# Another order of the action list in a one-core RetNet attention and GELU MLP kernel

## The chip, the core and the metric

The kernel runs on one core of a Trainium2 chip. The metric is the device time of one execution in microseconds (us). The profiler records one execution: every instruction of the engines PE (TensorE matmul), DVE (VectorE), ACT (ScalarE), POOL (GpSimd) and SP (SyncE), and the DMA queues.

## The reference, cut to what matters

```python
def _attn_ref(q, k, v):                       # (8, 8, 576, 64): batch, heads, positions, head size
    scores = (1 / np.sqrt(D_)) * np.matmul(q, k.transpose(0, 1, 3, 2))
    gamma = 1.0 - 2.0 ** (-5.0 - np.arange(H))
    Dmat = np.where(rel >= 0, gamma[:, None, None] ** rel[None, :, :], 0.0)   # rel = pos_i - pos_j
    return np.matmul(scores * Dmat[None], v)

def _moe_ref(x, w_in, w_out):                 # x (4608, 512), w_in (512, 2048), w_out (2048, 512)
    h = x @ w_in
    return (0.5 * h * (1.0 + erf(h * inv_sqrt2))) @ w_out

# reference: x = attention output, heads joined: (8 * 576, 512); out = _moe_ref(x, w_in, w_out)
```

## The kernel before

**Attention.** The 576 positions of a batch are cut into four chunks of 128 and a tail of 64. There are 36 units of 128 tokens (two tails share a unit) in 22 groups; from group 4 on a group holds the same chunk of two batches. For each group the actions are: `t` turns q and k on PE (groups 0 to 6), `d` turns them by a transposing DMA that SP issues (groups 7 to 21, two each); `s` is the score product, `m` the masking on DVE, `i` the product with v, `u` the running state of a pair of batches, `x` its cross term, `e` the eviction into the transposed activations. `v` scales the v tile, by DVE where its last figure is 0 and by eight ACT instructions where it is 1.

**MLP.** The 4608 tokens are nine blocks of 512. `1` is a tile of the first layer (blocks 0 to 4) with its GELU on ACT, `2` the second layer of block 0. From block 1 on the second layer is a Strassen-like scheme of seven products, written `p<block>.<product>.<quarter>`, each quarter four 128x256 matmuls; the products are M3, M4, M5, M1, M2, M6, M7 for figures 0 to 6. From block 5 on the first layer is such a scheme too (`f`). `G`, `W`, `I`, `J`, `X` are sums on DVE that prepare its operands.

**Loads and fillers.** `L<what>.<which>` issues a load on POOL's queue: 0 is q, 1 k, 2 v, 3 a quarter-pair of w_in, 4 of w_out, 5 the iota constants, 6 a step of the table dqT, computed on POOL. `C` casts the first q and k, `K` stores a kept row block of block 0. `w<n>` runs n matmuls on a tile of zeros; ten more of them stand ahead of the list. `Z` emits constants.

**The order.** Nothing is scheduled at run time. One list, `SEQ`, is walked from front to back and each action emits its instructions at once, so the list fixes the order on every engine's queue: PE's matmuls, POOL's load issues, SP's transposes and stores, DVE's and ACT's work. While it is walked, a table of expected times `T` is kept; the helper `either` uses it to put a copy on DVE or on ACT, and the banks of PSUM are picked by it. The buffers that the prediction needs are `qk` (five, one for a group from group 4 on; a load into one waits until the group that had it has been turned and its state formed), `v` (nine) and `qkT` (four).

**The end.** In the last block product M5 (`p8.2`) is copied to the right half of the output tile `lo` by `either`, and its two row blocks are stored from SP. M6 (`p8.5`) is finished on DVE in two steps; its stores are issued from ACT, SP and ACT. M7 (`p8.6`) is subtracted on DVE from M5's copy in three pieces, stored from SP, ACT, SP. The lines are:

```python
        elif p in (M5, M2):
            at = either(0.68, max(done, o_at(t, p == M2)), lo[:, :, RIGHT] if p == M5 else hi[:, :, LEFT], m)
...
                if last:
                    store(t, 2 + x, hi[:, x, RIGHT], 256, 512, nc.scalar, nc.sync)
...
            x, c0, c1 = PIECES[piece]
            nc.vector.tensor_tensor(lo[:, x, c0:c1], m[:, 0], lo[:, x, 256 + c0:256 + c1], op=MINUS)
...
            store(t, x, lo[:, x, c0:c1], c0, c1, nc.scalar if piece == 1 else nc.sync)
```

`store` counts its issue time for SP in the table of expected times, whichever engine issues it.

Of the kernel before, what the change touches and what calls it, by code (L numbers as in the profile page):

```python
# [17 lines left out]
def kernel(  # L18
# [47 lines left out]
    n = v_order.index(pair_of[0, NCI - 2][0])  # L66
    v_order[n:n] = kept

    N_PE_TR = 7
# [189 lines left out]

    def qk_free(n):  # L260
        g = groups[n]
        ends = list(sg[n]["ends"].values()) if "ends" in sg[n] else [sg[n]["T"]]
        assert len(ends) == 2 or n < N_PE_TR and sg[n]["halves"] == 4
        assert units[g[0]][2] is None or g[0] in s_done
        return max(ends + [st[g[0]].get("U", 0.0)])
# [253 lines left out]
    def scores(n):  # L519
        g = groups[n]  # L520
        qkT = sg[n]["qkT"]
        pe_waits(sg[n]["T"])
# [582 lines left out]
    for _ in range(N_WARM):  # L1105
# [3 lines left out]
    SEQ = ("L3.1 L1.1 L3.0 L5.0 L0.1 L2.0 L0.2 L1.2 C0.0 C1.0 t0.0.0 Z0 w2 L2.1 Z0 Z1 t0.1.0 Z0 w5 L3.2 Z1 s0 m0 L2.2 Z1 "  # L1109
# [109 lines left out]
```

## Time and profile before

| | us |
|---|---|
| median of 3 runs | 284.53 |
| lowest, highest | 284.08, 285.22 |
| the profiled execution | 284.17 |
| its span in the trace | 282.3 |
| PE busy in the span | 276.3 |
| DVE, ACT, POOL busy | 211.3, 152.6, 114.1 |

The profiled execution took 1.9 us more than its span, which lies around it, and 0.36 us less than the median. A PE row's end in the timeline is modelled and overlaps the next start; starts are recorded.

### The profile page before, as it was taken

What the parts mean: (1) busy time and instruction counts of PE and PEld (TensorE: products, weight loads), DVE (VectorE), ACT (ScalarE), POOL (GpSimd) and SP (SyncE); (2) the same over time, 40 slices, a digit from 0 to 9 for tenths busy, and PEclk for the clock granted to TensorE, in tenths of its full rate; (3) what the DMA queues carried; (4) which work ended last, traced back from release to release, by engine and by line L of the source; (5) the groups of instructions that cost most, each with busy time, mean ns of one, the idle gap of its engine ahead of it and who ended that gap; (6) DMA issues with size and microseconds to landing.
All of it is one profiled execution on the core that took longest, in us unless ns stands there. A gap on an engine that the chain in (4) does not pass through costs nothing.

```text
span 282.3 us, 8187 instructions
## 1 busy us (share of the span) xinstructions
PE 276.3 (98%) x3413; PEld 211.7 (75%) x3413; DVE 211.3 (75%) x413; ACT 152.6 (54%) x330; POOL 114.1 (40%) x143
## 2 busy tenths in 40 slices
PE   8999999999999999999999999999999999999994
PEld 3576777578874588547775588888888888888894
DVE  5662784886984775989749976898799989984852
ACT  5766745464156631575646565666584457765210
POOL 8987897907955447544076736000000000000000
PEclk9999999999999999999999999999999999999999
DMA  9999999999999999999999999960012013000035
GB/s 146 166 181 179 183 167 178 126 131 202 145 190 177 196 141 127 184 198 138 138 155 138 190 154 156 144 171 1 2 74 77 2 34 120 1 2 0 28 123 150
DMA packets 152804, 35.39 MB, mean 125 GB/s; under 512 B 141120, under 2 KB 148928, under 8 KB 152768
## 3 DMA queue, kind: packets, MB, share of 16 engines
q0 software_dynamic: 116832, 18.10, 101.2%
q1 hardware_dynamic: 34528, 16.26, 32.3%
q10 hardware_dynamic: 1408, 0.52, 0.8%
q8 instruction: 26, 0.43, 0.6%
q14 instruction: 10, 0.08, 0.1%
HBM read 36.70 MB, written 9.44 MB: 163 GB/s over the span
## 4 chain that ended last, share of the span: by engine, by line
PE 91%; POOL 4%; DMA 3%; issue 0%; DVE 0%; POOLq 0%
PE psum L948 35%; PE psum L762 23%; PE psum L1047 18%; PE psum L807 5%; PE psum L651 3%; PE psum L551 3%; DMA w_in<-in_moe_w_in_dram 3%; POOL qk L347 2%; PE psum L702 2%; PE psum L672 1%; POOL v_ld L347 1%; POOL w_in L306 1%; PE psum L499 1%; PE psum L538 0%; PE psum L637 0%
## 5 line engine op out<-in xcount | busy, mean ns | idle before, releaser
L762 PE MATMUL psum<-xT,w_in 128*128 128x512 bf16 (+3 forms) x504 | 74.1, 301 | 0.3 <-DMA w_in<-in_moe_w_in_dram 0.2
L948 PEld LDWEIGHTS <-gs 128*128 128x128 bf16 x656 | 62.3, 98 | 8.3
L771 ACT ACTIVATE g<-psum 128x512 bf16<-128x512 f32 (+2 forms) x91 | 49.6, 546 | 31.6 <-PE psum L762 27.2
L762 PEld LDWEIGHTS <-w_in 128*128 128x128 bf16 x504 | 42.6, 98 | 25.0 <-DMA w_in<-in_moe_w_in_dram 0.9
L948 PE MATMUL psum<-w_sum,gs 128*128 128x256 bf16 (+1 forms) x400 | 50.5, 268 | 0.0
L347 POOL DMA_DIRECT2D qk_ld<-in_k_dram x36 | 30.4, 850 | 29.4 <-DMA qkT<-qk_ld 18.6
L347 POOL DMA_DIRECT2D v_ld<-in_v_dram x40 | 34.3, 865 | 14.0 <-DMA qk_ld<-in_k_dram 5.3
L347 POOL DMA_DIRECT2D qk_ld<-in_q_dram x36 | 30.7, 863 | 15.7 <-DMA qkT<-qk_ld 7.1
L948 PE MATMUL psum<-w_out,gs 128*128 128x256 bf16 x256 | 33.9, 273 | 0.0
L1074 ACT ACTIVATE g<-psum 128x512 bf16<-128x512 f32 x48 | 27.0, 593 | 7.5 <-PE psum L1047 6.5
L948 PE MATMUL psum<-w_sum,g 128*128 128x256 bf16 x256 | 30.8, 273 | 0.0
L948 PEld LDWEIGHTS <-g 128*128 128x128 bf16 x256 | 24.7, 98 | 3.6
L1047 PEld LDWEIGHTS <-w_in 128*128 128x128 bf16 x256 | 24.9, 98 | 3.0
L845 DVE TENSOR_TENSOR gs<-g 128x1024 bf16<-128x1024 bf16 x32 | 21.7, 685 | 3.7 <-ACT g L771 3.1
L849 DVE TENSOR_TENSOR gs<-g 128x1024 bf16<-128x1024 bf16 x32 | 21.6, 684 | 1.4 <-ACT g L771 1.4
L614 ACT ACTIVATE vh<-v_ld,dv 128x64 bf16<-128x64 bf16 x88 | 22.0, 336 | 0.0
L1047 PEld LDWEIGHTS <-wi 128*128 128x128 bf16 x192 | 18.5, 98 | 2.4 <-issue 0.2
L1047 PE MATMUL psum<-xT,w_in 128*128 128x256 bf16 x128 | 19.2, 273 | 0.0
L1047 PE MATMUL psum<-xs,w_in 128*128 128x256 bf16 x128 | 18.9, 273 | 0.0
L1047 PE MATMUL psum<-xs,wi 128*128 128x256 bf16 x128 | 18.7, 273 | 0.0
L617 DVE TENSOR_TENSOR vh<-v_ld,dv 128x512 bf16<-128x512 bf16 x25 | 17.7, 712 | 0.4 <-DMA v_ld<-in_v_dram 0.4
L1070 ACT ACTIVATE g<-p 128x512 bf16<-128x512 f32 x16 | 10.1, 630 | 13.9 <-DVE p L1068 13.9
(101 smaller groups left out, 359.0 us busy)
## 6 DMA issues: line engine op xcount, KB each, us to landing
out_dram<-o SPq DMA_DIRECT2D x27, 256.0 KB, 5.1
v_ld<-in_v_dram POOLq DMA_DIRECT2D x32, 128.0 KB, 7.8
qk_ld<-in_k_dram POOLq DMA_DIRECT2D x28, 128.0 KB, 9.5
qk_ld<-in_q_dram POOLq DMA_DIRECT2D x28, 128.0 KB, 8.3
w_in<-in_moe_w_in_dram POOLq DMA_DIRECT2D x8, 256.0 KB, 7.2
w_out<-in_moe_w_out_dram POOLq DMA_DIRECT2D x8, 256.0 KB, 7.8
out_dram<-o SPq DMA_DIRECT2D x14, 128.0 KB, 2.0
v_ld<-in_v_dram POOLq DMA_DIRECT2D x8, 64.0 KB, 6.7
```

The costliest lines, as they stand in the source:

```text
L347: nc.gpsimd.dma_start(dst, src[2 * bp + jj, :, ci * C:ci * C + n, :].rearrange("h s d -> s h d"))
L614: nc.scalar.activation(vh[:, h, :], loaded[i][1][:, h, :], AF.Copy, scale=dv[:, h, ci:ci + 1])
L617: nc.vector.tensor_tensor(vh, loaded[i][1], dv[:, :, ci:ci + 1].to_broadcast([128, H, D]), op=ALU.mult)
L762: nc.tensor.matmul(hT[:, m, :], lhsT=w[:, cc, o:o + 128], rhs=x_tiles[t][:, cc, lo:hi], start=(cc == 0), stop=(cc == N_DM - 1))
L771: nc.scalar.activation(g_of(t, m0 // 2)[:, m0 % 2:m0 % 2 + n, lo:hi], hT, AF.Gelu)
L807: nc.tensor.matmul(oT, lhsT=g_of(t, m // 2)[:, m % 2, cols], rhs=w_out_sb[m // 2][:, m % 2, :], start=(m == 0), stop=(m == N_DF - 1))
L845: nc.vector.tensor_tensor(s.rearrange("p m a b -> p m (a b)"), g[:, :, 0, :], g[:, :, 1, :], op=ALU.add)
L849: nc.vector.tensor_tensor(s, g[:, :, :, LEFT], g[:, :, :, RIGHT], op=MINUS)
L948: nc.tensor.matmul(m[:, 0 if apart else ts, :], lhsT=a, rhs=w[:, c0:c1], start=p in begins and mm == 0 and ts == 0, stop=mm == N_DF // 2 - ...
L1047: nc.tensor.matmul(m[:, y, :], lhsT=a[:, c], rhs=d[:, c], start=p in (P1, P7) and y == 0 and c == 0, stop=c == 1, skip_group_check=True)
L1070: nc.scalar.activation(g[:, :, 1, RIGHT], v, AF.Gelu)
L1074: nc.scalar.activation(g[:, :, rows, cols], m, AF.Gelu)
```

## The change

`SEQ` is replaced by another list. The multiset of actions is the same but for two kinds. The old list holds six `w` actions, 19 matmuls on zeros (w2, w5, w7, w2, w2, w1); the new one has four, 16 matmuls (w2, w5, w7, w2). Twelve of the `v` actions change engine: 3, 5, 14, 22, 24, 28, 30, 32 and 33 go from ACT to DVE, and 6, 12 and 19 from DVE to ACT, so that DVE has six more of 36 and ACT six fewer. Everything else is order. A helper `turned` is added, which is only asserted. Cut to the stretches that the prediction speaks of:

```diff
+    def turned(n):
+        return len(sg[n].get("ends", ())) == 2 or sg[n].get("halves", 0) == (2 if n < 4 else 4)
...
-    SEQ = ("L3.1 L1.1 L3.0 L5.0 L0.1 L2.0 L0.2 L1.2 C0.0 C1.0 t0.0.0 Z0 w2 L2.1 Z0 Z1 t0.1.0 Z0 w5 L3.2 Z1 s0 m0 L2.2 Z1 "
-           "w7 L1.3 Z1 t1.0.0 L3.3 Z1 t1.1.0 w2 Z1 i0 L0.3 Z1 v0.0 x0 e0 w2 s1 m1 L2.3 t2.0.0 10.0.2.0.128 L3.4 t2.1.0 "
-           "10.2.2.0.128 L3.5 i1 x1 e1 w1 L3.6 s2 m2 10.4.2.0.128 L1.4 10.0.2.128.256 x3 10.2.2.128.256 10.4.2.128.256 "
-           "v1.0 u0.0 x2 i2 e2 10.6.2.0.256 t3.0.0 t3.1.0 10.2.2.256.384 10.6.2.256.384 10.0.2.256.384 L3.7 10.9.1.0.384 "
-           "10.8.1.0.384 s3 m3 10.10.1.0.384 10.11.1.0.384 10.12.1.0.384 L1.5 L0.5 i3 L0.4 10.13.1.0.384 10.15.1.0.384 e3 "
...
+    SEQ = ("L3.1 L1.1 L3.0 L5.0 L0.1 L2.0 L0.2 L1.2 C0.0 C1.0 t0.0.0 Z0 w2 L2.1 Z0 Z1 t0.1.0 Z0 w5 L3.2 s0 L2.2 t1.1.0 Z1 "
+           "Z1 m0 Z1 Z1 w7 L3.3 t1.0.0 L1.3 i0 L0.3 s1 Z1 w2 m1 Z1 e0 t2.0.0 t2.1.0 10.2.2.0.128 i1 s2 m2 e1 10.0.2.0.128 "
+           "10.4.2.0.128 v0.0 10.2.2.128.256 L3.4 10.0.2.128.256 L3.5 i2 10.4.2.128.256 10.6.2.0.256 e2 L3.6 t3.1.0 "
+           "10.4.2.256.384 10.2.2.256.384 t3.0.0 10.6.2.256.384 10.0.2.256.384 v1.0 s3 L2.3 10.8.1.0.384 10.9.1.0.384 m3 "
+           "10.11.1.0.384 10.10.1.0.384 10.12.1.0.384 i3 u0.0 L0.4 L0.5 e3 10.13.1.0.384 L1.4 L1.5 L4.0 L3.7 L4.1 "
...
+           "d15.0 p3.5.1 d16.1 p3.4.3 p3.5.2 d15.1 p3.5.3 e21 p3.6.3 i22 i23 u2.2 s15 x14 m25 e22 m24 e23 14.0.1.0.512 J0 "
...
-           "p8.5.0 p8.5.1 p8.5.2 p8.5.3 p8.6.0 p8.6.1 p8.6.2 p8.6.3").split()
+           "G8.1.1.2 p8.3.1 p8.4.0 p8.4.1 p8.3.2 p8.3.3 p8.2.1 p8.4.2 G8.3.1.0 p7.5.3 G8.3.1.2 p8.5.0 p8.2.2 p8.5.1 p8.4.3 "
+           "p8.5.2 p8.5.3 p8.6.0 p8.2.3 p8.6.1 p8.6.2 p8.6.3").split()
```

In the old list the end of block 8 reads `p8.3.3 p8.2.3 p8.4.2 p8.4.3 p8.5.0` and so on, as shown. Around the middle of the new list the loads stand in the order `L1.24 L1.27 L0.25 L2.25 L1.25 L0.24` and the transposes in the order `d14.1 d14.0 d16.0 d15.0 d16.1 d15.1`; in the old one the loads read `L0.24 L2.22 L0.25 L1.24 L1.25 L1.27` and the transposes `d14.0 d14.1 d15.0 d15.1 d16.0 d16.1`.

More of the change, by code (lines that the diff above doesn't have):

```diff
@@ L262, in qk_free @@
         ends = list(sg[n]["ends"].values()) if "ends" in sg[n] else [sg[n]["T"]]
-        assert len(ends) == 2 or n < N_PE_TR and sg[n]["halves"] == 4
+        assert turned(n)
         assert units[g[0]][2] is None or g[0] in s_done
@@ L521, in scores @@
         qkT = sg[n]["qkT"]
+        assert turned(n)
         pe_waits(sg[n]["T"])
```

112 rows, old and new, of the table SEQ are left out of this document.

## The prediction

> **What bounds the kernel now.** I read the page's first part and its chain first, then what PE waited for, then the stretches, then the opening and the end as timelines.
>
> ```profile
> span 282.3 us, 8187 instructions
> PE 276.3 (98%) x3413; PEld 211.7 (75%) x3413; DVE 211.3 (75%) x413; ACT 152.6 (54%) x330; POOL 114.1 (40%) x143
> ...
> PE 91%; POOL 4%; DMA 3%; issue 0%; DVE 0%; POOLq 0%
> ```
>
> PE is busy for 276.3 of 282.3 us and is 91% of the chain that ended last. A full engine can still hold stalls, so the waits of PE come next (waited for: us, times, longest):
>
> ```profile
> PE psum L1106 <- DVE zeros L119: 1.2, 1, 1.2
> PE psum L499 <- DMA qk<-in_q_dram: 0.7, 1, 0.7
> PE psum L672 <- DVE vh L617: 0.2, 1, 0.2
> PE psum L762 <- DMA w_in<-in_moe_w_in_dram: 0.2, 1, 0.2
> ```
>
> These four are all, and they lie in the opening: the stretches (columns: length, then busy time of PE, PEld, DVE, ACT, POOL, the granted clock, DMA) are full behind it.
>
> ```profile
> 21.30:40.00 18.70, 18.70 (x251) 12.75 (x250) 11.07 (x23) 10.89 (x28) 15.41 (x19) 1.00 1.91 178
> ...
> 278.65:282.30 3.65, 0.00 (x0) 0.00 (x0) 0.29 (x1) 0.00 (x0) 0.00 (x0) 0.96 0.53 149
> ```
>
> From 21.3 us PE is busy without a gap, and 3.65 us of drain follow the last matmul. So a new order can win only three things: time in the opening, matmuls that are not needed with the gaps that PE makes itself, and the drain. It can lose in any place where PE now never waits. The floor is close, since the products themselves are the same.
>
> **Term 1, the opening: three matmuls on zeros fewer, -0.65 us.**
>
> ```profile
> 7.99 1.68 PE L1099 MATMUL psum<-zeros 128*128 128x512 bf16 x7
> 10.34 0.62 PE L499 MATMUL psum<-ident,qk 128*128 128x128 bf16 x8 [0.67 <-DMA qk<-in_q_dram]
> 10.80 0.59 PE L1099 MATMUL psum<-zeros 128*128 128x512 bf16 x2
> 11.32 0.41 PE L651 MATMUL psum<-ret,v_ld 128*64 128x128 bf16 x8
> ```
>
> Seven matmuls on zeros last 1.68 us and two 0.59, so one costs (1.68 - 0.59)/5 = 0.22; three are 0.65. The 0.67 stays: q of unit 1 is the fourth load in both lists. The two waits of 0.2 go, since `u0.0` moves behind `i3` and w_in 4 to 6 come ahead of v3. In their place `i0` waits for v0, which cannot start before 11.32, and `t2.1.0`, `10.4.2.0.128` and `10.6.2.0.256` stand close to their loads. I book the exchange of waits at nothing, with 0.5 either way. The cover that must hold is the load order: v3, k5 and w_in 7 land later than before, and each must still land ahead of its use; if that cover goes, PE stands still for as long as the load is late.
>
> **Term 2, mode changes of PE, -0.45 us.**
>
> ```profile
> 30.51 0.89 PE psum L762 x16
> 31.40 0.57 PE psum L551 x32
> 31.97 1.00 PE psum L762 x16
> ```
>
> The same 16 matmuls take 0.11 us more behind a group of 64x64 matmuls, in the chain's rows. Counting changes between tile sizes in the built order gives 80 before and 76 after; 4 x 0.11 = 0.45.
>
> **Term 3, the end, +1.3 us.** This is where the lists differ most for their length. The last 7 us before:
>
> ```profile
> 274.67 1.07 ACT L474 COPY o<-psum 128x512 f32<-128x512 f32 x2
> 275.28 4.21 SPq L789 DMA_DIRECT2D out_dram<-o  x8
> 275.83 2.80 PE L948 MATMUL psum<-w_sum,gs 128*128 128x256 bf16 x32
> 276.96 0.76 DVE L897 SCALAR_TENSOR_TENSOR o<-psum,o 128x256 f32<-128x256 f32 x2 [2.08 <-PE psum L948]
> 277.42 1.77 ACTq L789 DMA_DIRECT2D out_dram<-o  x3
> 277.77 0.74 DVE L906 TENSOR_TENSOR o<-psum,o 128x256 f32<-128x256 f32 x2
> 278.67 0.29 DVE L906 TENSOR_TENSOR o<-psum,o 128x128 f32<-128x128 f32 x1 [0.15 <-PE psum L948]
> ```
>
> ```profile
> 85.25 0.44 PE psum L948 x4
> ```
>
> Call Z the modelled end of the last matmul, 278.63 here. Before, M5 and M2 are copied by ACT at 274.67, long before M6's subtraction (276.96) and ACT's three store issues (277.42, 1.77 us, 0.59 each). After, the last quarter of M5, `p8.2.3`, stands behind M6's last, `p8.5.3`, with three quarters of M7 behind it. The built order puts M5's copy on ACT **behind two of ACT's three store issues**, and M5's two stores on SP ahead of the last two pieces. In the opening ACT's next instruction starts only when its DMA issue is over:
>
> ```profile
> 0.74 0.49 ACTq L117 DMA_DIRECT2D first<-in_k_dram  x1
> 1.26 1.28 ACT L129 ACT_TABLE_LOAD   x1 [1.26 <-PEq L1203]
> ```
>
> So, with 0.44 us for a quarter: M6 ends five quarters before the end instead of four, and its subtraction starts at 276.96 - 278.63 - 0.44 = Z-2.1. ACT's first issue starts 0.46 later (277.42 against 276.96), Z-1.6, and two issues last to Z-0.5. The copy (1.07/2, about 0.55) ends at Z+0.1. The first piece needs it: Z+0.2 to Z+0.6 on DVE; the two others, 0.29 each, end at Z+1.1, where before they ended at 278.96 = Z+0.3. SP's eight issues take 4.21, 0.53 each: M5's two from Z+0.2 to Z+1.2, the first piece to Z+1.8, the last to Z+2.3; before, the eighth ended at 279.49 = Z+0.9. That is +1.4; if DVE alone set it, +0.8. I take +1.3, range 0.7 to 1.5, nearer the queue because all eight rows show it.
>
> [...]
>
> **Term 4, a late transpose in the middle, +0.5 us.** Loads and transposes, issue durations (min/median/max ns), then us to landing:
>
> ```profile
> L347 POOL DMA_DIRECT2D qk_ld<-in_k_dram x36: 679/883/967, 16.0 to 168.2; - x36
> ...
> DMA to landing us min/median/max: 4.0/8.5/14.2
> ```
>
> ```profile
> L510 SPq DMA_TRANSPOSE qkT<-qk_ld x30: 1193/1900/4187, 54.0 to 187.0; - x30
> ...
> DMA to landing us min/median/max: 4.2/7.9/11.7
> ```
>
> ```profile
> 119.28 0.64 PE L651 MATMUL psum<-ret,v_ld 128*64 128x128 bf16 x16
> ...
> 120.10 0.64 PE L551 MATMUL psum<-qkT 64*64 64x128 bf16 x32
> 120.67 7.94 PE L762 MATMUL psum<-xT,w_in 128*128 128x512 bf16 x36
> ...
> 145.25 0.64 PE L551 MATMUL psum<-qkT 64*64 64x128 bf16 x32
> ```
>
> The 120.10 row is `s13`, right behind `u2.0`; the 145.25 row is `s15`. Between them PE had 25 us of work. In the new list the load `L1.27` must wait for `u2.0` to free its buffer, and v25, k25 and both halves of q for `s15` are queued behind it on POOL; before, they were ahead. What remains between `u2.0` and `s15` is 28 quarters (0.44), six 512-column tiles (7.94/9, 0.87) and two blocks of attention (119.28 to 120.67, 1.4 each): 12.3 + 5.2 + 2.8 = 20.3 us. Within it must fit: four issues of 0.88 ahead of q24, its landing, two transposes issued ahead of the last, and that one's landing. With minima, 3.5 + 4.0 + 2.4 + 4.2 = 14.1; with medians of landing, 3.5 + 8.5 + 2.4 + 7.9 = 22.3; with the slowest, 31.8. The cover holds below 20.3. POOL has been held up before, so the queue is short then, which favours values below the medians. I take a wait of 0.5, between none (14.1) and 2.0 (22.3).
>
> The engine changes of `v` I cost at nothing: DVE, 75% busy, gets six more of 36, ACT is relieved, and behind the opening PE waits for neither now. PSUM banks, the sums (`G`, `W`, `I`, `J`, `X`) and `K` I cost at nothing too: counted in the lists with the durations above, the shortest stretch of PE work between a score product and its use is 3.3 us (2.2 before), between a first-layer tile and the product that reads it 1.3 (1.3 before), and those pass without a wait. Where such a stretch is short by a copy, it costs some 0.3 us.
>
> **Sum.** 284.17 (the profiled execution: span 282.3 and 1.9 around it) - 0.65 - 0.45 + 1.3 + 0.5 = 284.9. The profiled execution lies 0.36 below the median of the runs, 284.53, so this is 0.4 to 0.7 above no change. 0.5%, 1.42 us, is about what a measurement of this kernel can tell from no change; 285.95 and 283.11 are the bounds.
>
> **Rivals.**
> - *Forecast: the end gives back what the opening gains.* 284.9, with its own range 283.9 to 285.9. Chance 0.55.
> - *Slower: the transposes for `s15` set the time.* For: medians alone make PE 2.0 late. Against: the list before has similar chains and no wait. With landings at 10 us each, 3.5 + 10 + 2.4 + 10 = 25.9, 5.6 late; 284.4 without term 4, so 286.4 to 290.0, typically 287. It decides once the last transpose lands 21.9 us after `u2.0`, a wait of 1.6. Chance 0.27.
> - *The gain stands: the end is not longer*, because SP or ACT issue faster or the drain hides it. 284.17 - 1.1 = 283.1, which straddles the bound for faster. For: DMA moves little there. Against: ACT's in-order issue. Chance 0.10.
> - *The change does not do what it says in the opening*: idle time only moves, since v3, k5 and w_in 7 come late and term 1 is lost. 284.9 + 0.65 = 285.5. Chance 0.08.
>
> **Numbers.** Predicted 284.9. The range leaves out about a tenth at each end: below, part of the third case, so 283.3; above, the worse half of the second, so 287.3. Faster: half of the third case, 0.05. Slower: the second case and 0.03 of the others, 0.30. Same: 0.65.
>
> **What would show it.** Three L1099 fewer and the timeline full from about 21 us half a us to one us ahead in work; the end of the last matmul about a us earlier; in the last stretch ACT's copy (L477 in the new file) behind two store issues, the first L910 half a us after the last matmul, the drain about 5 us instead of 3.65; in PE's waits a line for scores (L555) on `qkT` near 146 us of 0 to 2 us. A drain of 3.65 or less, a PE wait of over 2 us anywhere behind 21 us, or an opening that is later, would make the prediction wrong.

## The result, and the profile after

The new list takes 294.03 us (median of 4 runs, 291.05 to 296.85) where the old one took 284.70 beside it (4 runs, 284.08 to 285.22): 1.029 times as long, 95% interval 1.021 to 1.038. The prediction was 284.9, 283.3 to 287.3. The ratios here leave out runs more than 1.5% above the fastest of their kernel; where waits vary from run to run that can leave out ordinary long runs too, so medians and ranges of all runs stand beside them. The profiled run of the new list is its longest, 296.85. Its page (the span, PE's line, the clock in 40 slices, the engines in the chain that ended last) and the first line of what PE waited for:

```profile
span 295.1 us, 8145 instructions
...
PE 279.1 (95%) x3410; PEld 214.1 (73%) x3410; DVE 213.7 (72%) x414; ACT 140.9 (48%) x282; POOL 113.9 (39%) x143
...
PEclk9999999999999899999999969999999999999999
...
PE 55%; DMA 30%; POOL 10%; issue 2%; SPq 1%; ACT 0%; DVE 0%; DVEq 0%; POOLq 0%
```

```profile
PE psum L555 <- DMA qkT<-qk_ld: 8.6, 4, 4.3
```

PE's share of the chain fell from 91% to 55%, DMA's rose from 3% to 30%. PE was full behind 21 us before; now it stands still four times there, for 8.6 us in all, each time for a DMA transpose that a score product (`s`) needs. PE's timeline has the four rows, `s9`, `s10`, `s15`, `s17` (start, duration, and in brackets the idle time before):

```profile
81.30 0.64 PE L555 MATMUL psum<-qkT 64*64 64x128 bf16 x32 [0.78 <-DMA qkT<-qk_ld]
...
100.95 1.07 PE L555 MATMUL psum<-qkT 64*64 64x128 bf16 x32 [2.62 <-DMA qkT<-qk_ld]
...
153.20 0.64 PE L555 MATMUL psum<-qkT 64*64 64x128 bf16 x32 [0.88 <-DMA qkT<-qk_ld]
...
170.40 1.07 PE L555 MATMUL psum<-qkT 64*64 64x128 bf16 x32 [4.33 <-DMA qkT<-qk_ld]
```

Behind the two long waits the same 32 matmuls take 1.07 us instead of 0.64: the granted clock has halved. The stretches show where (length, busy time of PE, PEld, DVE, ACT, POOL, then the clock, DMA, GB/s):

```profile
97.00:100.42 3.42, 1.33 (x49) 1.08 (x49) 1.03 (x2) 1.18 (x2) 0.00 (x0) 1.00 1.71 152
100.42:103.83 3.41, 2.88 (x41) 2.18 (x41) 1.77 (x3) 0.00 (x0) 1.65 (x2) 0.50 0.94 186
165.27:168.68 3.41, 0.80 (x4) 0.18 (x2) 0.41 (x1) 0.73 (x2) 1.45 (x3) 1.00 1.98 126
168.68:172.10 3.42, 1.71 (x66) 1.61 (x67) 0.53 (x1) 0.00 (x0) 1.25 (x3) 0.50 2.74 134
172.10:175.51 3.41, 3.41 (x18) 2.43 (x17) 3.22 (x7) 0.64 (x2) 2.01 (x3) 0.50 1.63 161
```

At half clock PE worked from 100.95 to 103.83 and from 170.40 to 175.51; half of that, 1.44 + 2.55 = 3.99 us, would be lost if every matmul there took twice as long. Starts give a little less: from `s10` to `s12` the new list took 20.64 us and from `s17` to `s18` 27.38, where the same PE work at full clock took 19.28 (d10 moved, below) and 25.03 (d17 moved): 1.36 + 2.35 = 3.71 us.

**The sum.** The two profiled executions differ by 296.85 - 284.17 = 12.68 us. Waits 8.61, half clock 3.99, a longer drain 0.95, less 0.70 that the opening gained (counted by the columns that the matmuls of both records had put through, the new list is some 0.6 to 0.7 us ahead where the old one stands at 40, 60 and 80 us), less 0.10 around the span: 12.75; with 3.71 for the half clock, 12.47. Either closes to 0.2 us or better.

**Why the transposes are late.** For `s10`, the old list's PE, DVE and SP, then the new list's:

```profile
78.16 1.91 PE L948 MATMUL psum<-w_sum,gs 128*128 128x256 bf16 x16
...
80.17 0.69 DVE L897 SCALAR_TENSOR_TENSOR o<-psum,o 128x512 f32<-128x512 f32 x1 [0.47 <-issue]
...
80.89 1.20 SPq L789 DMA_DIRECT2D out_dram<-o  x2
...
82.25 7.91 SPq L510 DMA_TRANSPOSE qkT<-qk_ld  x3
```

```profile
79.50 8.36 SPq L793 DMA_DIRECT2D out_dram<-o  x6
...
85.34 0.60 PE L952 MATMUL psum<-w_sum,gs 128*128 128x256 bf16 x4
...
86.30 0.68 DVE L901 SCALAR_TENSOR_TENSOR o<-psum,o 128x512 f32<-128x512 f32 x1
...
88.02 13.61 SPq L513 DMA_TRANSPOSE qkT<-qk_ld  x6
```

and the flight of its last transpose in the chain of waits:

```profile
89.67 11.24 DMA qkT<-qk_ld
```

The matmul row in each of the two views ends with `p1.5.3`; DVE subtracts, SP issues the two stores of the result (in the new list the last two of six that began at 79.50), and only then d10's transposes. Loads are not what they wait for: in the new list the last of q15, q16, k15, k16 (the loads of group 10) landed at 82.2, 5.8 us before the first issue. From DVE's start to the last landing the way is as long as before: 80.17 to 94.59 (14.4 us) and 86.30 to 100.91 (14.6). What shrank is the PE work that covers it. Before, `p1.5.3` ended at 80.07 and `s10` began at 95.93, 15.9 us later; after, it ended at 85.94 and `s10` was due at 100.95 - 2.62 = 98.33, 12.4 us later. For `s17`, DVE and SP, then the last transpose's flight in the chain:

```profile
151.77 0.68 DVE L915 TENSOR_TENSOR o<-psum,o 128x512 f32<-128x512 f32 x1
...
151.88 2.77 SPq L793 DMA_DIRECT2D out_dram<-o  x4
...
154.83 17.02 SPq L513 DMA_TRANSPOSE qkT<-qk_ld  x4
```

```profile
157.44 12.81 DMA qkT<-qk_ld
```

Four stores of `p3.5.3` and `p3.6.3` are ahead, though all loads of this group had landed at 144.2; 12.8 us after its issue the last transpose lets `s17` start. Counted in the lists, the PE work between the last step with stores ahead of a transpose and its product was at least 15.1 us in the old list for groups 10 to 17, and is 12.4 (s10), 12.6 (s13), 13.7 (s14) and 13.7 (s17) in the new one. The cover alone does not decide: `s13` and `s14` did not wait. From the end of that step to the last landing the way was 15.0 us for d10 and 18.7 for d17, but 8.8 for d13 and 6.5 for d14, whose transposes landed 3.3 to 5.0 us after their issue. The DMA column of the stretches (the packets' time as a share of 16 engines' time, which can pass 1) reads 1.0 while d13 and d14 were under way, 1.9 for d10 and 2.2 for d17.

`s15` is the chain of term 4, in POOL's timeline and the chain of waits:

```profile
132.35 0.88 POOL L350 DMA_DIRECT2D qk_ld<-in_k_dram  x1 [16.42 <-PE psum L676]
```

```profile
144.78 8.38 DMA qkT<-qk_ld
```

POOL stood 16.42 us at `L1.27`, for `u2.0`; `s15` came 0.88 late. The 0.78 us at `s9` are neither: no store is ahead of d9, SP issued four transposes back to back from 62.05 to 74.28, and the last landed 10.7 us after its issue, at 81.16.

**The end**, in the timeline of all engines:

```profile
286.66 5.91 SPq L793 DMA_DIRECT2D out_dram<-o  x10
...
288.38 0.76 DVE L901 SCALAR_TENSOR_TENSOR o<-psum,o 128x256 f32<-128x256 f32 x2 [1.19 <-ACT o L477]
...
288.84 1.20 ACTq L793 DMA_DIRECT2D out_dram<-o  x2
289.00 1.49 PE L952 MATMUL psum<-w_sum,gs 128*128 128x256 bf16 x20
290.15 0.58 ACT L477 COPY o<-psum 128x512 f32<-128x512 f32 x1 [2.11 <-DMA out_dram<-o]
290.77 0.82 DVE L910 TENSOR_TENSOR o<-psum,o 128x256 f32<-128x256 f32 x3 [1.63 <-ACT o L477]
```

Z, the modelled end of the last matmul, is 290.49. Two store issues of ACT start at Z-1.65, its copy runs to Z+0.24, DVE ends at Z+1.1; the drain, from there to the end of the span, is 295.1 - 290.49 = 4.6 us against 3.65.

### The profile page after: what moved, and what is told of

It reads as the page before. It is cut to its first block, busy times and chain, and to the rows that moved or that the text cites. A ratio compares the mean times of both kernels' runs of the same rounds, so it can differ in the third digit from the quotient of the medians.

```text
span 295.1 us, 8145 instructions
## 1 busy us (share of the span) xinstructions
PE 279.1 (95%) x3410; PEld 214.1 (73%) x3410; DVE 213.7 (72%) x414; ACT 140.9 (48%) x282; POOL 113.9 (39%) x143
## 4 chain that ended last, share of the span: by engine, by line
PE 55%; DMA 30%; POOL 10%; issue 2%; SPq 1%; ACT 0%; DVE 0%; DVEq 0%; POOLq 0%
PE psum L952 27%; PE psum L1051 17%; DMA qkT<-qk_ld 11%; PE psum L766 6%; DMA v_ld<-in_v_dram 6%; DMA w_out<-in_moe_w_out_dram 5%; DMA qk_ld<-in_q_dram 5%; POOL v_ld L350 3%; DMA qk_ld<-in_k_dram 2%; POOL qk_ld L350 2%; PE psum L555 2%; POOL w_in L309 2%; POOL qk L350 2%; PE psum L655 1%; SPq L513 1%
## 5 line engine op out<-in xcount | busy, mean ns | idle before, releaser
L766 PEld LDWEIGHTS <-w_in 128*128 128x128 bf16 x504 | 43.0, 98 | 24.2
L952 PE MATMUL psum<-w_sum,gs 128*128 128x256 bf16 (+1 forms) x400 | 52.0, 269 | 0.0
L350 POOL DMA_DIRECT2D v_ld<-in_v_dram x40 | 34.4, 879 | 10.9 <-DMA v_ld<-in_v_dram 2.7
L952 PE MATMUL psum<-w_out,gs 128*128 128x256 bf16 x256 | 35.2, 273 | 0.0
L952 PE MATMUL psum<-w_sum,g 128*128 128x256 bf16 x256 | 34.5, 285 | 0.0
L952 PEld LDWEIGHTS <-g 128*128 128x128 bf16 x256 | 25.8, 102 | 5.0 <-issue 0.2
L1051 PEld LDWEIGHTS <-w_in 128*128 128x128 bf16 x256 | 25.3, 99 | 3.3
L592 DVE TENSOR_TENSOR ret<-psum,msk 128x1024 bf16<-128x1024 f32 x16 | 19.3, 1219 | 5.4 <-PE psum L555 5.4
L621 DVE TENSOR_TENSOR vh<-v_ld,dv 128x512 bf16<-128x512 bf16 x31 | 20.9, 684 | 0.0
L555 PE MATMUL psum<-qkT 64*64 64x128 bf16 x448 | 9.8, 232 | 8.6 <-DMA qkT<-qk_ld 8.6
```

Source lines behind the costliest of these rows:

```text
L350: nc.gpsimd.dma_start(dst, src[2 * bp + jj, :, ci * C:ci * C + n, :].rearrange("h s d -> s h d"))
L555: nc.tensor.matmul(got[j][h % 2][1][cols, h // 2, :], lhsT=qkT[sl, 1, h, cols], rhs=qkT[sl, 0, h, :], start=(h < 2), stop=True, skip_group ...
L592: nc.vector.tensor_tensor(r.rearrange("p e h q -> p (e h) q"), both_of(got[0][0], HP), by, op=ALU.mult)
L621: nc.vector.tensor_tensor(vh, loaded[i][1], dv[:, :, ci:ci + 1].to_broadcast([128, H, D]), op=ALU.mult)
L766: nc.tensor.matmul(hT[:, m, :], lhsT=w[:, cc, o:o + 128], rhs=x_tiles[t][:, cc, lo:hi], start=(cc == 0), stop=(cc == N_DM - 1))
L952: nc.tensor.matmul(m[:, 0 if apart else ts, :], lhsT=a, rhs=w[:, c0:c1], start=p in begins and mm == 0 and ts == 0, stop=mm == N_DF // 2 - ...
```

## The experiments

Theory A: transposes stand on SP behind stores that wait for DVE, with too little PE work left to cover the way. Theory B: the DMA engines are full, and loads and transposes come late in whatever order. Theory C: opening and end lose the time.

**d10 ahead of its two stores.** Only POOL's and SP's places change; PE's order is the same.

```diff
 L2.14 v14.0
+L1.16 L2.15 L0.15 L0.16 d10.1 d10.0
 p1.5.3 12.13.1.0.512
...
-L1.16
...
-L2.15
...
-L0.15 L0.16 d10.1
...
-d10.0
```

> The new list with the transposes d10.1 and d10.0 (and the four loads L1.16, L2.15, L0.15, L0.16 that stood between) moved ahead of p1.5.3, so that on SP's queue they stand ahead of that step's two stores; the order on PE is the same. Theory A (transposes wait on SP behind stores that wait for DVE): the loads had landed at 82.2 us, the issue starts about there instead of at 88.0, lands 5 us sooner, PE's wait of 2.6 us at s10 goes and with it the 1 us of half-speed matmuls behind it: about 290.5 us (289.5 to 291.5) against 294.0. Theory B (the DMA engines are full, and a transpose lands when they get to it): s10 comes at most 1 us earlier, 293 to 294. Theory C (the loss is in opening and end): no change, 294.

Measured: 293.33 us (287.91 to 296.53), ratio 1.018 (1.012 to 1.025). In the profile the two transposes issue from 80.8 instead of 88.0, land by 94.9 instead of 100.9, and `s10` does not wait: that part of A held, and it is the place on SP that did it, since the four loads that move along issue within 1 us of where they did. The time did not follow: the median lies above A's range and in B's, since other products became late. PE's timeline:

```profile
128.02 0.64 PE L555 MATMUL psum<-qkT 64*64 64x128 bf16 x32 [2.36 <-DMA qkT<-qk_ld]
...
169.94 1.07 PE L555 MATMUL psum<-qkT 64*64 64x128 bf16 x32 [5.79 <-DMA qkT<-qk_ld]
```

`s13`, with 3.8 us to spare in the new list, is now 2.36 late. PE comes to it 4.9 us earlier; d13, behind the stores of `p2.5.3`, is issued 4.3 to 5.0 us earlier too, but its halves take 10.7 and 10.0 us to land instead of 5.0 and 4.5, and so lands 1.2 us later than before.

**d17 ahead of its four stores.**

```diff
 p3.5.2 d15.1
+L2.24 L0.27 L1.28 L0.28 d17.1 d17.0
 p3.5.3
...
-L2.24 L0.27
...
-L1.28 d17.1 L0.28
...
-d17.0
```

> The new list with d17.1 and d17.0 (and the loads L2.24, L0.27, L1.28, L0.28 ahead of them) moved to stand right behind d15.1, ahead of the four stores of p3.5.3 and p3.6.3 on SP's queue; the order on PE is the same. Theory A: they issue at about 147 instead of 154.8 and 157.4 us, land near 160, and the wait of 4.3 us at s17 goes with the 2 us of slow matmuls behind it: 294.0 - 6.5 = 287.5 (286.5 to 289). Theory B (landing is what is slow, 12 us after issue in a burst of loads): landing at 159 to 165 still, the wait falls by half or more: 288 to 291. Theory C: 294.

Measured: 289.99 us (287.62 to 291.52), ratio 1.019 (1.014 to 1.025). The transposes issue at 147.9 and land at 158.0, 9.4 us ahead of `s17`. This wait is gone as A has it. The median lies above A's range and in B's: the gain fell 2.5 us short of A's, in its profile because `s10` still waits 2.90 with two stretches of half clock behind it instead of one, and `s15` 1.41.

**L1.27 behind L0.24.**

```diff
-L1.27 p3.6.0 L0.25
+p3.6.0 L0.25
...
-L0.24 I7
+L0.24 L1.27 I7
```

> The new list with the load L1.27 moved from ahead of L0.25 to behind L0.24, so that L0.25, L2.25, L1.25 and L0.24 no longer stand behind its wait for u2.0; nothing else moves. Theory A: POOL issues them near 116 us instead of 133 to 137, d15 lands long before s15, the wait of 0.9 us there goes; s17 is as late as before, since SP's queue is the same: 293.0 (292.5 to 293.7). Theory B: the loads of 132 to 145 us are spread, the transposes behind them land sooner too, and s17's wait of 4.3 shrinks: 288 to 292. Theory C: 294.

Measured: 292.23 us (291.11 to 294.04), ratio 1.030 (1.026 to 1.034). q24 and the three loads ahead of it issue at 114.6 to 117.1, `s15` has 6.4 us to spare. The wait at `s15` is gone as A has it. The time lies between A's range and B's. `s10` waits 2.90 and `s17` 2.68 (4.33 in the new list; d17's last transpose landed 10.9 us after its issue instead of 12.8), so something of B is in the size of `s17`'s wait, not in its existence, as far as one profile of each can tell.

**All three.**

> All three edits together. Theory A: the waits at s10, s15 and s17 go, 0.8 at s9 stays: 294.0 - 3.5 - 6.5 - 1.0 = 283.0, plus or minus what is late next: 282.5 to 285.5, the level of the kernel before (284.7). Theory B: 286 to 290. Theory C: 294, since opening and end are as in the new list.

Measured: 289.72 us (288.11 to 292.93), ratio 1.017 (1.014 to 1.021). The time lies in B's range, 4 us above A's upper end, though the waits at `s10` and `s17` are gone as A has it; `s13` is what is late next:

```profile
129.19 1.07 PE L555 MATMUL psum<-qkT 64*64 64x128 bf16 x32 [3.43 <-DMA qkT<-qk_ld]
```

d13's loads had all landed by 113.3; SP issued the three stores ahead of it from 113.97 and d13 at 115.98 and 117.94. So 2.7 us of the delay are A's mechanism a third time. The rest is landing: 9.9 and 11.2 us for these two, with a DMA column of 2.0, against 5.0 and 4.5 in the new list. The edits of one place so leave both accounts standing, and ask for an edit that takes all places at once.

**All stores of blocks 1 to 3 behind the transposes.** The stores are held in the program until the next group's two transposes have been issued, or until the next block writes to the same tile (whose allocation moves there); `L1.27` is moved as above and `d15.1` ahead of `d16.1`:

```diff
-                store(t, 2 + x, hi[:, x, :])
+                store_late(t, 2 + x, hi[:, x, :])
...
+    def store_late(t, *a):
+        held_stores.append((t, *a))
+        if t > 3:
+            store_held()
...
     for x in SEQ:
         perform(x[0], [int(y) for y in x[1:].split(".") if y])
+        if x[0] == "d" and len(sg[int(x[1:].split(".")[0])]["ends"]) == 2:
+            store_held()
```

> The new list with L1.27 behind L0.24, with d15.1 ahead of d16.1, and with the stores of blocks 1 to 3 held back in the program until the next group's two transposes have been issued (they stand behind those on SP's queue instead of ahead). Theory A (SP's stores ahead of the transposes): d10, d13 and d17 issue as soon as their loads are there; no wait at s10 and s17, s13 0.6 us (its loads landed 2.7 us before its issue in the kernel with all three edits, where it was 3.3 late), 0.7 at s9, no half clock: 284.2 - 0.7 - 0.5 + 1.0 + 1.3 = 285.3 (284.3 to 286.5). Theory B (loads and transposes share full DMA engines, whatever the order on SP): one wait goes and the next comes, with a half clock: 287.5 to 290.

Measured: 285.25 us (10 runs, 284.42 to 287.81), ratio 1.0037 (1.0008 to 1.0066). A said 285.3, B 287.5 to 290. No line that waits for a DMA into `qkT` is left among the waits of PE; those over half a us:

```profile
PE psum L1123 <- DVE zeros L119: 1.2, 1, 1.2
PE psum L555 <- DVE xT L740: 1.0, 1, 1.0
PE psum L655 <- DMA v_ld<-in_v_dram: 0.6, 1, 0.6
```

The order of work on PE is that of the new list (a few copies went to the other of DVE and ACT). So nearly all of the 9.3 us were the places of transposes and of one load, on SP and POOL; the transposes still took up to 12.3 us to land, but no longer set the time. Of the 0.4% that stay, the profile shows 1.0 us of a wait for DVE and the drain of 4.7 us.

**The last copy early, on top of that.**

```diff
 p7.5.3 G8.3.1.2
+p8.2.2 p8.2.3
 p8.5.0
-p8.2.2
...
-p8.2.3
```

> The same kernel with p8.2.2 and p8.2.3 also moved ahead of p8.5.0, so that ACT's last copy stands ahead of its store issues and M5's two stores come early on SP. The time from the last matmul to the end falls by 1 us, to 3.9 as in the kernel before: 284.3 (283.3 to 285.5), 1.0 less than the kernel without it. Rival: SP's eight issues or the drain of the transfers set the end all the same: no change against it.

Measured: 285.55 us (6 runs, 284.73 to 286.11), ratio 1.0031 (1.0009 to 1.0053): no gain that can be told, as the rival has it. ACT's copy does run ahead of its stores, and the drain is 4.25 us instead of 4.73, half of what was expected; the profiled run had a wait of 1.8 us at `s14` that the one without the edit had not.

**The old list with d17 late.**

```diff
-p3.6.0 d17.0 p3.4.3
+p3.6.0 p3.4.3
...
-L1.31 d17.1 u2.2
+L1.31 u2.2
...
 p3.6.3
+d17.0 d17.1
```

> The old list with one thing of the new: d17.0 and d17.1 stand behind p3.6.3 (they stood ahead of p3.4.3 and behind p3.5.3), so that four stores are ahead of them on SP and 12.2 us of PE work are left between p3.6.3 and s17. Theory A: the way from such a step over DVE, the stores, two transposes and the landing took 15 to 18 us, so s17 waits 3 to 6 us, and the clock halves behind it for another 1.5 to 3: 289 to 292.5. Theory B (this place alone does no harm where the loads are spread as in the old list): 284 to 285.5.

Measured: 293.04 us (292.70 to 295.51), ratio 1.032 (1.027 to 1.036), half a us above A's range. One misplaced pair of transposes makes the old list as slow as the new one:

```profile
146.78 6.66 SPq L789 DMA_DIRECT2D out_dram<-o  x4
153.62 18.28 SPq L510 DMA_TRANSPOSE qkT<-qk_ld  x5
```

```profile
168.96 1.07 PE L551 MATMUL psum<-qkT 64*64 64x128 bf16 x32 [7.70 <-DMA qkT<-qk_ld]
```

The wait, 7.70 us, is longer than the 3 to 6 expected: from 153.62 on SP issues five transposes in 18.28 us, and the first two took until 160.4 to issue.

**Matmuls on zeros in the waits**, first 5 and 12, then 10 and 18.

```diff
-L2.16 s10
+L2.16 w5 s10
...
-v26.0 s17
+v26.0 w12 s17
```

> The new list with five matmuls on zeros ahead of s10 and twelve ahead of s17 (1.1 and 2.6 us), which lie within the waits of 2.6 and 4.3 us there. If the granted clock halves because PE stands still, the clock stays at 1.0, the waits with the matmuls in them are as long as before, and the half-speed stretches behind them (4.1 us in the profiled run) go: 290 to 291.5 against 294.0. If the clock has another cause: 294, with the same half-speed stretches.

> The new list with ten matmuls on zeros ahead of s10 and eighteen ahead of s17 (2.2 and 3.9 us), so that PE is busy for most of both waits. Across the profiles so far the clock halved for the next 3.41 us whenever PE had been busy for 0.36 or less of a stretch of 3.41 us, and not at 0.39 or more. If that is the rule, the clock stays at 1.0 between opening and end, the waits cost their own 8.6 us alone, and the time is 290.5 to 292.5. Rival (the clock has another cause): stretches at half clock stay, 293.5 to 295.

Measured: 294.42 us (293.47 to 294.89) and 294.60 (293.64 to 294.97). With 5 the clock still halved behind `s10` (PE busy 1.40 us of that stretch); with 12 it stayed at `s17`. With 10 and 18 it stayed at 1.0 from the opening to the end, as expected; its stretches around `s10` and `s17`:

```profile
96.66:100.07 3.41, 3.25 (x59) 1.93 (x58) 1.62 (x3) 1.78 (x3) 0.00 (x0) 1.00 1.85 153
100.07:103.48 3.41, 2.85 (x50) 2.01 (x48) 1.26 (x2) 0.00 (x0) 0.00 (x0) 1.00 1.52 148
164.92:168.33 3.41, 3.41 (x19) 1.62 (x18) 0.76 (x2) 1.09 (x2) 0.68 (x1) 1.00 2.01 111
```

The expected time did not come; both medians lie about where the rivals put them. In the last profile the zeros ran 1.1 us past the landing of d17 (168.8), `s15` waited 1.63 instead of 0.88, and the drain was 5.3. The runs do lie closer, within 1.4 us against 5.8 in the new list, though with four each. So the cause of the half clock is shown in these profiles: PE's idle time, 2.09 of 3.42 us in the stretch ahead of the half clock at `s10` in the new list (busy 1.33), 0.16 and 0.56 of 3.41 in the two around `s10` here. Its price shows in the trace alone: with the clock kept, `s10` to `s12` took 19.31 us and `s17` to `s18` 25.02 (20.64 and 27.38 in the new list), and what that saved went elsewhere.

**The opening alone, the end alone, the three matmuls alone**, each put into the old list.

```diff
-w2 Z1 i0 L0.3
+Z1 i0 L0.3
...
-e1 w1 L3.6 s2
+e1 L3.6 s2
```

> The old list with three of the 19 matmuls on zeros taken out (the two ahead of i0 and the one ahead of s2), nothing moved. As the prediction's first term has it, three at 0.22 us are gained: 284.5 - 0.65 = 283.85. Rival: the two ahead of i0 only fill the time until v0 lands (i0 started 0.06 us after that), so PE waits instead, and the gain of the new opening comes from its other order: 284.3 to 284.5.

> The old list with the new list's opening: its first 66 actions beside the matmuls on zeros (to v1.0, s3, L2.3 and two first-layer tiles, PE's first 22 us, with 16 matmuls on zeros instead of 19), then the old list's other actions in their own order. Theory: the opening gains what it gains in the new list, where PE was 0.7 us ahead from 40 to 78 us: 284.5 - 0.7 = 283.8 (283.5 to 284.2). Rival: s9 had its transpose only 0.32 us ahead in the old list, so PE comes too early there and half the gain is lost as a wait: 284.2 to 284.5.

> The old list up to its last 128 actions beside the matmuls on zeros (from f7.2.0 on), then the new list's order for those, p8.2.3 late. Theory (the end as in the new list: ACT's copy behind two store issues): 4.9 us from the last matmul to the end instead of 3.9: 284.5 + 1.0 = 285.5 (285.1 to 285.8). Rival: the end of the new list is longer only because its last loads and stores came late: no change, 284.5.

(The diff is that of the three matmuls; the two others are splices of the lists.) Measured, against 284.31 for the old list (29 runs): three matmuls fewer 285.43, ratio 1.002 (0.9997 to 1.004); the new opening 285.05, 1.001 (0.999 to 1.003); the new end 285.14, 1.0026 (1.0001 to 1.005). The first two medians lie above forecast and rival alike. Without the three, PE waits where they were, in its timeline:

```profile
9.98 0.62 PE L499 MATMUL psum<-ident,qk 128*128 128x128 bf16 x8 [0.30 <-DMA qk<-in_q_dram]
...
10.95 0.41 PE L651 MATMUL psum<-ret,v_ld 128*64 128x128 bf16 x8 [0.34 <-DMA v_ld<-in_v_dram]
```

With the whole new opening PE reaches `s9` 0.44 us earlier (80.62 against 81.06) and loses it at `s10`, whose transpose landed at 96.0 there (94.6 in the old list's profile):

```profile
96.08 0.64 PE L551 MATMUL psum<-qkT 64*64 64x128 bf16 x32 [0.52 <-DMA qkT<-qk_ld]
```

The end alone: a drain of 4.6 us in place of 3.65, and 0.8 us in the median, with an interval that only just lies above 1. Its profiled run, at 287.43 the longest of 12, also had a wait for w_in of 1.4 us in the opening and a stretch of half clock behind it.

## Why the prediction was wrong

- **Term 1, -0.65: the size came true inside the new list (some -0.6 to -0.7 by 80 us), its reason did not.** The three matmuls alone bring nothing, as the rival case "idle time only moves" has it, so the right size was luck. With the whole new opening in the old list PE is 0.44 us early at `s9`, and that too does not reach the end.
- **Term 2, -0.45 for mode changes: not seen, and not excluded.** The sum above closes to 0.2 us without it, but the half clock in it is only known to 0.3, and no run takes the four changes alone.
- **Term 3, +1.3 for the end: the steps came as forecast, a third too large, and they are only part of the cause.** Each step is in the rows: issues from Z-1.65 (predicted Z-1.6), copy to Z+0.24 (Z+0.1), DVE's end Z+1.1 (Z+1.1). The drain grew by 0.95, between the value for DVE alone (0.8) and that for SP's eight issues (1.4), and by as much with the new end alone in the old list. But with the copy ahead of ACT's issues half of it stayed (4.25 us against 3.65); what sets that half is open.
- **Term 4, +0.5 for `s15`: right, 0.88, and far too narrow. This is the step that failed.** The text said of the new order that it "can lose in any place where PE now never waits", then looked only at the one chain with a load that waits. Every transpose that the new list puts closer behind a store was such a place, and two cost 2.6 and 4.3 us. The old trace held the price: d10's last landing (94.59) came 14.5 us behind the end of `p1.5.3` (80.07), `s10` 15.9 behind it. With 12.4 us left in the new list the same way is 2.1 us too long, where 2.62 was measured. That rule finds the places, not the sizes: it would call `s13`, `s14` and `s17` late by 1.9, 0.8 and 0.8 us, and they waited 0, 0 and 4.33. SP's queue was weighed for the end alone, and the waits of transposes behind stores were so put at nothing without a reason; they cost 6.95 of the 8.61 us, and `s9` 0.78 more.
- **"Against: the list before has similar chains and no wait"** was weak evidence, since it did not count what cover those chains had: for transposes behind stores at least 15.1 us of PE work.
- **The clock was not in the sum at all.** Nearly a third of the loss, 3.7 to 4.0 us, is half clock behind the two waits. The rival for `s15` priced a late transpose by its wait alone.
- What would show it wrong: "a PE wait of over 2 us anywhere behind 21 us" is what came, twice.

Not settled: why the new list with all transposes early still lies 0.3 to 0.4% above the old one, beyond the drain and the wait for DVE that one profile shows; and no version beat the old list.

## What to carry to other kernels

Where one engine's queue carries stores that wait for results and transposes that others wait for, list for every transpose the last waiting store ahead of it, and compare the work left until its product with the whole way in the old trace: wait, store issues, transpose issues, landing. The way itself ran from 6.5 to 18.7 us here, so take its long end, not one value. A full bottleneck engine that never waits says nothing about how much cover is left; when a wait is cured, look at once which cover it had given to the next one. Price a wait of the matmul engine with the half-clock stretch that can follow it (3.41 us behind the wait of 2.62 and 6.83 behind that of 4.33 in the new list).

## What the runs showed of the hardware

In the profile of the new list the granted clock changes, between the opening and the drain, at 100.42, 103.83, 168.68 and 175.51 us; the steps between are 3.41, 64.85 and 6.83 us, or 1, 19 and 2 times 3.41. The edges differ from run to run: a stretch begins at 97.00 there, at 98.16 with five matmuls on zeros ahead of `s10` and at 96.66 with ten. Waits shorter than 3.41 us stood ahead of a halving: 2.62 us in the new list, of which 2.09 lay in one stretch (PE busy 1.33 of 3.42 us there), and 2.02 us with the five matmuls on zeros (1.40 of 3.42). With L1.27 moved, a wait of 2.68 us at `s17` fell across two stretches and the clock stayed:

```profile
161.96:165.38 3.42, 2.21 (x13) 0.98 (x10) 1.82 (x4) 1.79 (x3) 1.35 (x2) 1.00 2.06 141
165.38:168.79 3.41, 1.93 (x74) 1.82 (x75) 1.18 (x2) 0.00 (x0) 1.36 (x2) 1.00 1.88 147
```

Over these profiles it halved behind stretches with PE busy for 0 (the old list with d17 late) to 1.49 of 3.41 us (d17 moved), and once at 1.73 (the new end alone, 16.02 to 19.43, in the opening); it stayed at 1.60 and 1.73 (with matmuls on zeros in the waits) and above, and once at 1.45 (the old list with d17 late, 288.70 to 292.11, at its end), so these figures bound no sharp threshold (busy as the view has it; the expectation above counted a matmul only up to the start of the next, which gives lower shares; by the view the stretch at 97.00 has 0.39 and halved). It came back behind a stretch with 2.88 us busy (the new list), not behind one with 1.71 (the same) or 2.44 (d17 moved). Waits of like length so cost unlike sums: by the starts of `s10` and `s12`, `s10`'s wait of 2.62 to 2.90 us cost 1.4, 1.7 and 2.8 us more in three profiles, and the 2.68 us at `s17` cost nothing more. That may be one source of the new list's spread of 5.8 us; only one of its runs has a trace.

SP issued in the order of the list: d10's loads had landed at 82.2, and its transposes issued at 88.0 behind two stores that waited for DVE, but at 80.8 where the list has them ahead. A transpose's issue on SP took from 1.19 to 4.52 us in the new list (1.19 to 4.19 in the old one), and its landing came from 2.7 to 12.1 us after the issue's start (12.8 for d17's last, in the chain of waits). The long landings go with a busy DMA column: of the 24 transposes whose landing the trace of the new list has, the ten with a column of at most 1.22 from issue to landing took 2.7 to 5.0 us, the fourteen with 1.55 or more 5.2 to 12.1.
